# One mask for both halves of a tile, the exponential behind the routing matmuls, earlier routing for tiles 12 to 15, paired scatters

## The chip, the cores and the metric

One core of a Trainium2 chip runs the whole program in one launch. Its engines are TensorE (PE: matmuls; PEld: the weight loads in front of them), VectorE (DVE), ScalarE (ACT), GpSimd (POOL) and SyncE (SP), which issues most DMAs; POOL issues the indirect ones. Each engine works through its own list of instructions in the order in which the program wrote them. The metric is the device time of one execution in microseconds (us). The profile has a second number of this kind, the time of the profiled execution.

## The reference

Three layers follow each other over 4 x 768 tokens with 384 channels (8 heads of 48).

```python
for t in range(S):                      # attention with a decaying state, per batch and head
    cur = u * k[t] (x) v[t]
    y[t] = r[t] . (state + cur)
    state = w * state + k[t] (x) v[t]
# first mixture of experts: tokens with x @ w_skip > 0 only, the others pass unchanged
e = argmax(x @ w_gate);  gate = softmax(x @ w_gate)[e]
x = x + gate * (relu(x @ w1[e]) @ w2[e])
# second mixture of experts: every token, no residual
out = gate2 * (relu(x @ w1b[e2]) @ w2b[e2])
```

Each mixture has 8 experts of 384 x 1024 and 1024 x 384.

## The kernel before

**Attention.** The 3072 tokens are 24 tiles of 128, tile n from 0 to 23; a tile is an even and an odd chunk of 64 tokens, which lie on different partitions. XE[n % 4] and XO[n % 4] are two buffers of 128 partitions. For the even chunk, XE holds the decayed r in partitions 64 to 111, and XO is to hold the masked score matrix in 64 to 127; for the odd chunk it is the other way round. prep_a(n) (L535) makes the decayed k (KTL, L539) and r (XE, L543, both chunks at once) on DVE and r times k (RKP, L544) on POOL. prep_b(n) (L546) copies the odd chunk's r from XE into XO on ACT. amat(n) is four steps: the score matmuls (amat_a, L584 and L585, both chunks into one PSUM tile a_ps), the matmuls for the diagonal (amat_q, L593), and mask (L595), which multiplies the two halves of a_ps by a triangle, one DVE instruction into the lower half of XE and one into the upper half of XO. prep_kq (L556) makes KDE, KDO and qv on DVE. uy (L604) is the recurrence: it updates the state with one chunk and makes the output of the chunk before, uy even with XO (L617, L621) and uy odd with XE (L615, L623). evac_state (L625) copies the state from PSUM on ACT: L631 after uy even, L629 after uy odd. finish (L633) adds qv to the output on DVE. In iteration n of the loop, the program writes uy even (n), prep_a(n+3) with finish(n-1) in its middle, amat(n+2), prep_kq(n+2), uy odd (n), prep_b(n+3), and then the gate's logits of tile n-2 (gate_l, L271) and transposes of tile n-1 (gate_x, L396).

**Routing.** route (L285) turns logits into a slot for each token: transposes (L296), nine or ten small DVE steps up to the one-hot matrix ohm (L327) and its sum cs (L332), the exponential on ACT (L334), three DVE steps to the gate weight, matmuls that count the tokens ahead (rk, L344 to L348), three DVE steps to the index and the running count cum (L350 to L354). It is a generator: it yields the name of an engine, and the loop calls tick at fixed places, which lets it write its next instruction. A slot is half an iteration (in the experts: one piece of a matmul job). The first number behind the engine's name is a lag in slots; a step of another engine has lag 1 if none is given. GROUPS says which tiles are routed together and with which lag; with burst, all DVE and ACT steps that follow each other are written at one tick. Only one generator runs at a time, others queue.

**Rows to the experts.** A routed tile is scattered to its experts' rows in DRAM by indirect DMA on POOL (L276). Tiles 0 to 15 fill the first 160 rows of expert 0: in iteration 21, early_rows writes what is left of their routing, the scatters of those tiles and, behind them on POOL, the load of these rows (L933). first_T transposes them (L943) and first_1 (L949) begins the experts.

**Experts.** Jobs 0 to 7 are the first mixture's experts, job 8 and 9 the second mixture's expert 0 in two parts, then the rest. A job has slots k = 0 to 15: eight of gemm1 (L1077) and eight of gemm2 (L1100). When a job of the first mixture is done, gate_rows routes its rows for the second one during the next job; send2 issues its two scatters, one a slot. Three row buffers go round, so a load of new rows (L1040) waits until the scatters of the rows in that buffer have landed. Rows of the eighth job go into job 9, whose transposes (L1052) come from slot 13 of job 8 on.

Of the kernel before, what the change touches and what calls it, by code (L numbers as in the profile page):

```python
# [52 lines left out]
FILL = (17, {}, 6)  # L53
W_LO, W_HI = 0.7, 1.5

GROUPS = {0: (4, 2), 4: (4, 2), 8: (4, 2), 12: (4, 2), 16: (4, 0), 20: (3, 1), 23: (1, 1)}
LL, LT0 = 5, 13
PF2 = range(8, 23)
PF1 = (3, 4, 5, 6, 7, 8)
# [123 lines left out]
def attn_moe_moe_kernel(ctx: ExitStack, tc: tile.TileContext, t, out):  # L183
# [101 lines left out]
    def route(lt, X, g0, n, two, idx_out, ec):  # L285
# [43 lines left out]
        if n > 1:  # L329
            cs = rt_p.tile([128, nc_], F32, tag="cs", name="cs")  # L330
            yield "dve"
            V.tensor_reduce(out=cs, in_=ohm.rearrange("p g c -> p c g"), axis=AX.X, op=ALU.add)  # L332
        yield "act0"
        A.activation(out=ex, in_=lm, func=ACTF.Exp)  # L334
        sm = rt_p.tile([128, n, sets, 1], F32, tag="sm", name="sm")
        yield "dve0"
        V.tensor_reduce(out=sm, in_=ex, axis=AX.X, op=ALU.add)
        yield "dve"
        V.tensor_scalar(out=sm, in0=sm, scalar1=1e-9, scalar2=None, op0=ALU.add)
        yield "dve"  # L340
        V.reciprocal(out=X[:, g0:g0 + n, G1 + (0 if two else 1):G2 + 1], in_=sm.rearrange("p g s o -> p g (s o)"))
        sl = rt_p.tile([128, n, nc_], F32, tag="sl", name="sl")
        yield "pe 0" if two or len(whole) > E - 2 else "pe 3"
        T.matmul(rk, lhsT=ones[0:2, :], rhs=ecap[:, ec, c0:16].unsqueeze(1).to_broadcast([2, n, nc_]), start=True, stop=False)  # L344
        T.matmul(rk, lhsT=ones, rhs=cum[:, c0:16].unsqueeze(1).to_broadcast([128, n, nc_]), start=False, stop=False)
        for g in range(n - 1):
            T.matmul(rk[:, g + 1:n], lhsT=ones, rhs=ohm[:, g].unsqueeze(1).to_broadcast([128, n - 1 - g, nc_]), start=False, stop=False)
        T.matmul(rk, lhsT=tri, rhs=ohm, start=False, stop=True)  # L348
        yield "dve"
        V.scalar_tensor_tensor(out=sl.rearrange("p g c -> p (g c)"), in0=ohm.rearrange("p g c -> p (g c)"), scalar=-NOSLOT, in1=rk.rearrange("p g c -> p (g c)"), op0=ALU.mult, op1=ALU.add)  # L350
        yield "dve"
        V.tensor_reduce(out=idx_out.unsqueeze(3), in_=sl.rearrange("p g (s c) -> p g s c", c=8), axis=AX.X, op=ALU.min)
        yield "dve"
        V.tensor_tensor(out=cum[:, c0:16], in0=cum[:, c0:16], in1=cs, op=ALU.add)  # L354


    gens = []
# [51 lines left out]
    def attention():  # L409
        with ExitStack() as actx:  # L410
# [58 lines left out]
            def fl(x):  # L469
                return x.rearrange("p h c -> p (h c)")  # L470
# [74 lines left out]

            def prep_b(n):  # L546
                x = n % NX
                A.copy(out=fl(XO[x][0:D]), in_=fl(XE[x][0:D]))

            def prep_v(n):  # L550
                A.copy(out=fl(VSO[n % NL][64:128]), in_=fl(VSE[n % NV][64:128]))
# [17 lines left out]
                tick("dve")  # L569
                qv_t[n] = qv  # L570

            a_t = {}

            def amat(n):
                amat_a(n)
# [3 lines left out]
            def amat_a(n):  # L579
                x = n % NX  # L580
                a_ps = ps.tile([128, H, C], F32, tag="a", bufs=2, name="a_ps")
                kt_ = ktil.pop(n)
                for h in range(H):
                    T.matmul(a_ps[0:64, h], lhsT=kt_[64:128, h], rhs=XE[x][64:128, h], start=True, stop=True)  # L584
                    T.matmul(a_ps[64:128, h], lhsT=kt_[0:48, h], rhs=XO[x][0:48, h], start=True, stop=True)  # L585
                a_t[n] = a_ps

            def amat_q(n):
# [6 lines left out]
            def mask(n):  # L595
                x = n % NX
                a_ps = a_t.pop(n)
                for X, r0 in ((XE[x], 0), (XO[x], 64)):
                    V.tensor_tensor(out=X[r0:r0 + 64], in0=a_ps[r0:r0 + 64], in1=before[r0:r0 + 64].to_broadcast([64, H, C]), op=ALU.mult)
                    tick("dve")  # L600

            y_ps, u_ps = {}, {}

# [49 lines left out]
            def gate_l(n):  # L653
                g0, gn, k = grp[n]
                if k == 0:
                    lt_t[g0] = ps_g.tile([128, 512], F32, tag="lt", name="lt_ps")
                lt_ps = lt_t[g0]
                logits_T(lt_ps[:, k * 128:k * 128 + 128], xT_t.pop(n), 128)
                if k == gn - 1:
                    lt = ga_p.tile([96, 512], F32, tag="lt", bufs=2, name="lt")  # L660
                    defer.append(lambda: A.copy(out=lt[:, 0:gn * 128], in_=lt_ps[0:96, 0:gn * 128]))
                    if g0 >= EARLY:
                        deferred()
                    busy.add(g0)
                    start(gate_route(lt, g0, gn), lag=GROUPS[g0][1], burst=g0 == 20)

            busy = set()

# [57 lines left out]
            prep_kq(0)  # L726
            setup5(2)
            zero_state(0)
            fill(FILL[2])
            load_rk(3)  # L730
            load_kv(3)
            for n in range(NT):
# [3 lines left out]
                deferred()  # L736
                if n == 0:
                    prep_v(1)
                slot[0] += 1
                tick("pe ")  # L740
                fill(FILL[1].get(n, 0))
# [46 lines left out]
                if n == 0:  # L788
                    amat_a(2)
                    amat_q(2)  # L790
                    prep_a(3)
                    mask(2)
                    prep_kq(2)
                    load_rk(5)
                if n + 3 < NT:
                    prep_b(n + 3)
                    prep_v(n + 3)
# [339 lines left out]
    def work(j, k):  # L1137
# [14 lines left out]
            tick("dve")  # L1152
        if j <= E:
            if j > 1:
                send2(1 + (j == E))
            if skipped and j > 2 and k % 2 == 0:
                g = skipped.pop(0)
                scatter(xs2, idx_all[:, g, 1:2], xall[:, g], SLOTS2 - 1, "s2")
# [137 lines left out]
```

## Time and profile before

| | us |
|---|---|
| median of 3 runs | 582.07 (581.66 to 582.59) |
| the profiled execution, its own time | 586.06 |
| span of its instructions | 584.3 |
| attention, from the first uy even to the last logits | 18.8 to 157.2 |
| first expert's matmuls begin | 166.5 |
| mean granted TensorE clock, share of full speed | 0.969 |

A row of the timeline has start, duration, engine, line, operation, what it writes and reads, how many instructions are merged, and in brackets the idle time of the engine before it with what ended it. The clock has two levels, 1.2 and 2.4 GHz; a clock of 0.75 in a stretch says that it was at the lower level for half of it.

### The profile page before, as it was taken

To read this page: it belongs to the slowest core of one execution; us is meant where nothing else is said; L and a number is where in the kernel's file an instruction comes from. 1 tells how busy PE (TensorE), PEld (TensorE's weight loads), DVE (VectorE), ACT (ScalarE), POOL (GpSimd) and SP (SyncE) were. 2 spreads that over 40 slices of the span, in tenths; PEclk is the share of its full clock that TensorE was granted. 3 is DMA by queue.
4 is the path that set the end of the run, shared out by engine and by line. 5 is a ranking of instruction groups with operands and counts; after the bars stand their busy time and mean duration, and the time that the engine had idled before them with its cause. 6 is when DMAs were issued, how large, how long until landed. Compare 5 with 4: busy or idle time off the path is not lost. (4 is left out here: it accounts for less than half of the span.)

```text
span 584.3 us, 14702 instructions
## 1 busy us (share of the span) xinstructions
PE 551.1 (94%) x5947; PEld 496.8 (85%) x5948; DVE 361.2 (62%) x761; ACT 266.1 (46%) x536; POOL 207.6 (36%) x224
## 2 busy tenths in 40 slices
PE   6999898898789999999999999999999999999992
PEld 4788797787677899998989799988989898999992
DVE  7999999999536577766775536444434344455210
ACT  6344444544325654654465326443445354555320
POOL 6442234432342233688733322222231313141301
PEclk8779898999979999999999999999999999999997
DMA  7959777887523756687766533766465564742100
GB/s 153 212 144 272 233 222 206 251 271 282 191 92 113 275 174 218 203 256 227 257 207 214 165 106 111 242 206 212 165 200 167 182 231 145 260 144 81 38 16 27
DMA packets 57661, 107.67 MB, mean 184 GB/s; under 512 B 7321, under 2 KB 40958, under 8 KB 57584
## 3 DMA queue, kind: packets, MB, share of 16 engines
q1 hardware_dynamic: 51584, 94.57, 52.9%
q0 software_dynamic: 6000, 12.07, 5.6%
q8 instruction: 49, 0.80, 0.6%
q14 instruction: 28, 0.23, 0.1%
HBM read 85.86 MB, written 26.91 MB: 193 GB/s over the span
## 5 line engine op out<-in xcount | busy, mean ns | idle before, releaser
L1077 PE MATMUL g<-xh,w1h 128*128 128x240 f32 (+7 forms) x384 | 121.3, 316 | 0.0
L1077 PE MATMUL g<-xl,w1h 128*128 128x240 f32 (+7 forms) x384 | 118.6, 309 | 0.1
L1077 PE MATMUL g<-xh,w1l 128*128 128x240 f32 (+7 forms) x384 | 118.5, 309 | 0.0
L1079 DVE SCALAR_TENSOR_TENSOR hl<-g,hh 128x384 fp32r<-128x384 f32 (+5 forms) x128 | 58.7, 464 | 85.2 <-ACT hh L1078 85.1
L1100 PE MATMUL g<-w2h,hh 128*128 128x384 f32 (+4 forms) x312 | 108.5, 348 | 0.0
L1100 PE MATMUL g<-w2h,hl 128*128 128x384 f32 (+4 forms) x312 | 105.0, 337 | 0.0
L1100 PE MATMUL g<-w2l,hh 128*128 128x384 f32 (+4 forms) x312 | 105.0, 336 | 0.0
L1078 ACT ACTIVATE hh<-g 128x384 fp32r<-128x384 f32 (+5 forms) x128 | 53.4, 417 | 62.8 <-PE g L1077 61.7
L887 POOL TENSOR_TENSOR w1l<-s,w1h 128x1024 fp32r<-128x1024 f32 x14 | 33.5, 2394 | 125.5 <-issue 106.6
L1077 PEld LDWEIGHTS g<-xh,w1h 128*128 128x128 f32 x384 | 72.6, 189 | 4.2 <-DVE w1l L887 2.5
L1077 PEld LDWEIGHTS g<-xl,w1h 128*128 128x128 f32 x384 | 72.6, 189 | 1.2 <-DVE xl L1056 0.3
L1077 PEld LDWEIGHTS g<-xh,w1l 128*128 128x128 f32 x384 | 72.6, 189 | 0.9
L276 POOL DMA_INDIRECT xs<-xall,idx_all x48 | 54.3, 1130 | 31.0 <-DVE cum L354 12.8
L1100 PEld LDWEIGHTS g<-w2h,hh 128*128 128x128 f32 (+4 forms) x312 | 57.6, 185 | 4.0 <-issue 3.0
L276 POOL DMA_INDIRECT out<-rows,ids x30 | 29.1, 971 | 85.3 <-ACT rows L921 59.8
L1100 PEld LDWEIGHTS g<-w2l,hh 128*128 128x128 f32 (+4 forms) x312 | 57.1, 183 | 0.7
L1100 PEld LDWEIGHTS g<-w2h,hl 128*128 128x128 f32 (+4 forms) x312 | 56.9, 182 | 0.8
L544 POOL TENSOR_TENSOR RKP<-RK 112x512 f32<-112x512 f32 x22 | 29.7, 1348 | 74.4 <-DMA RK<-in_rk 58.0
L1056 DVE TENSOR_TENSOR xl<-xt_ps,xh 128x240 fp32r<-128x240 f32 (+7 forms) x48 | 23.0, 478 | 49.3 <-ACT xh L1055 49.2
L887 DVE TENSOR_TENSOR w1l<-s,w1h 128x1024 fp32r<-128x1024 f32 x28 | 34.4, 1230 | 21.3 <-ACT w1h L886 21.3
L887 DVE TENSOR_TENSOR w2l<-s,w2h 128x1152 fp32r<-128x1152 f32 x28 | 37.9, 1354 | 13.4 <-ACT w2h L886 13.4
L886 ACT CAST w2h<-s 128x1152 fp32r<-128x1152 f32 (+1 forms) x42 | 43.9, 1048 | 0.0
(200 smaller groups left out, 1053.2 us busy)
## 6 DMA issues: line engine op xcount, KB each, us to landing
s<-in_w1b SPq DMA_DIRECT2D x24, 512.0 KB, 3.8
s<-in_w1a SPq DMA_DIRECT2D x21, 512.0 KB, 3.9
RK<-in_rk SPq DMA_DIRECT2D x48, 192.0 KB, 4.0
KV<-in_kv SPq DMA_DIRECT2D x24, 384.0 KB, 5.1
s<-in_w2b SPq DMA_DIRECT2D x16, 576.0 KB, 4.8
s<-in_w2a SPq DMA_DIRECT2D x14, 576.0 KB, 5.8
w2r<-in_w2b SPq DMA_DIRECT2D x5, 1536.0 KB, 9.1
xs<-zrow SPq DMA_DIRECT2D x29, 194.0 KB, 4.6
```

What stands on the lines that cost most here:

```text
L276: i = P.indirect_dma_start(out=dst, out_offset=bass.IndirectOffsetOnAxis(ap=idx_col, axis=0), in_=src, in_offset=None, bounds_check=last, ...
L544: (V if n < 2 else P).tensor_tensor(out=RKP[x][0:112], in0=RK[i][:, 0], in1=RK[i][:, 1], op=ALU.mult)
L886: A.copy(out=hi, in_=x)
L887: (P if j in POOL_LO else V).tensor_tensor(out=lo, in0=x, in1=hi.bitcast(F32), op=ALU.subtract)
L1056: V.tensor_tensor(out=lo, in0=tp[:, 0:cap], in1=hi.bitcast(F32), op=ALU.subtract)
L1077: T.matmul(p, lhsT=a[:, kb, f], rhs=b[:, kb], start=(kb == 0 and i == 0), stop=(kb == KB - 1 and i == 2))
L1078: A.activation(out=hh[:, fb], in_=p[:, 0:full], func=ACTF.Relu)
L1079: V.scalar_tensor_tensor(out=hl[:, fb], in0=p[:, 0:full], scalar=0.0, in1=hh[:, fb].bitcast(F32), op0=ALU.max, op1=ALU.subtract)
L1100: T.matmul(p[0:m], lhsT=a[:, fb, r], rhs=b[:, fb], start=(fb == 0 and x == 0), stop=(fb == FB - 1 and x == 2))
```

## The change

mask writes both halves with one DVE instruction into XO; a new step mask_b copies the lower half from XO to XE and then the odd chunk's r into XO, both on ACT. The odd chunk's r now waits in a small tile xt (three buffers), which prep_b fills, and the odd score matmuls read XE. mask_b(n+2) is written behind uy odd (n) and its evacuation. In route, the matmuls rk come behind cs, then the exponential, then the index steps, then the three steps of the gate weight. The seventh expert's rows take the lag of 3 slots in front of rk that the earlier ones take. Group 12 gets lag 0 and burst. send2 issues two scatters in a slot for jobs 2 to 7 too.

```diff
-GROUPS = {... 12: (4, 2), 16: (4, 0), 20: (3, 1), 23: (1, 1)}
+GROUPS = {... 12: (4, 0), 16: (4, 0), 20: (3, 1), 23: (1, 1)}
...
-        yield "act0"
-        A.activation(out=ex, in_=lm, func=ACTF.Exp)
-        sm = ...
-        yield "dve0"
-        (sum of ex; + 1e-9; reciprocal)
         sl = rt_p.tile([128, n, nc_], F32, tag="sl", name="sl")
-        yield "pe 0" if two or len(whole) > E - 2 else "pe 3"
+        yield "pe 0" if two or len(whole) > E - 1 else "pe 3"
         (matmuls rk)
-        yield "dve"
+        yield "act0"
+        A.activation(out=ex, in_=lm, func=ACTF.Exp)
+        yield "dve0" if two and g0 >= EARLY else "dve"
         (sl, idx, cum)
+        yield "dve"
+        (sum of ex; + 1e-9; reciprocal)
...
             def prep_b(n):
                 x = n % NX
-                A.copy(out=fl(XO[x][0:D]), in_=fl(XE[x][0:D]))
+                xt_t[n] = wk.tile([64, H, C], F32, tag="xt", bufs=3, name="xt")
+                A.copy(out=fl(xt_t[n]), in_=fl(XE[x][0:64]))
...
-                    T.matmul(a_ps[64:128, h], lhsT=kt_[0:48, h], rhs=XO[x][0:48, h], start=True, stop=True)
+                    T.matmul(a_ps[64:128, h], lhsT=kt_[0:48, h], rhs=XE[x][0:48, h], start=True, stop=True)
...
-                for X, r0 in ((XE[x], 0), (XO[x], 64)):
-                    V.tensor_tensor(out=X[r0:r0 + 64], in0=a_ps[r0:r0 + 64], in1=before[r0:r0 + 64].to_broadcast([64, H, C]), op=ALU.mult)
-                    tick("dve")
+                V.tensor_tensor(out=XO[x], in0=a_ps, in1=before.to_broadcast([128, H, C]), op=ALU.mult)
+                tick("dve")
+                tick("dve")
+
+            def mask_b(n):
+                x = n % NX
+                A.copy(out=fl(XE[x][0:64]), in_=fl(XO[x][0:64]))
+                A.copy(out=fl(XO[x][0:64]), in_=fl(xt_t.pop(n)))
...
-                    start(gate_route(lt, g0, gn), lag=GROUPS[g0][1], burst=g0 == 20)
+                    start(gate_route(lt, g0, gn), lag=GROUPS[g0][1], burst=g0 in (12, 20))
...
+                if n + 2 < NT:
+                    mask_b(n + 2 if n else 1)
...
-                send2(1 + (j == E))
+                send2(2)
```

mask_b(0) is written ahead of the loop and mask_b(2) near the start of iteration 1.

## Rows read from the trace of the kernel before

**Rows 1.** The page: busy time of each engine, share of the span, instructions.
```profile
PE 551.1 (94%) x5947; PEld 496.8 (85%) x5948; DVE 361.2 (62%) x761; ACT 266.1 (46%) x536; POOL 207.6 (36%) x224
```

**Rows 2.** Windows by stage: stretch, length, busy time by engine, clock, DMA, GB/s.
```profile
59.37:83.33 23.96, 22.29 (x559) 19.79 (x559) 23.40 (x47) 10.51 (x23) 7.51 (x6) 0.93 0.77 229
...
107.48:131.59 24.11, 21.20 (x559) 18.59 (x559) 23.54 (x49) 10.56 (x23) 8.95 (x8) 1.00 0.91 273
131.59:157.23 25.64, 23.95 (x580) 20.57 (x579) 21.52 (x60) 10.34 (x23) 7.59 (x8) 1.00 0.67 236
157.23:166.48 9.25, 3.80 (x19) 2.32 (x19) 0.90 (x6) 1.67 (x4) 3.02 (x5) 0.75 0.50 166
```

**Rows 3.** Windows of single iterations: n = 8, 14, 15, 17 and 20.
```profile
66.08:72.92 6.84, 6.84 (x144) 6.16 (x144) 6.60 (x15) 3.04 (x7) 1.27 (x1) 0.75 0.71 215
102.03:107.48 5.45, 5.45 (x143) 4.79 (x142) 5.38 (x9) 3.63 (x8) 2.87 (x3) 1.00 0.65 208
107.48:114.74 7.26, 5.04 (x138) 4.42 (x137) 7.09 (x17) 2.00 (x6) 3.16 (x3) 1.00 0.92 274
...
120.39:125.36 4.97, 4.97 (x139) 4.42 (x138) 4.88 (x11) 2.98 (x6) 1.67 (x2) 1.00 0.97 288
...
138.44:143.78 5.34, 5.34 (x144) 4.71 (x144) 5.12 (x14) 3.04 (x7) 0.00 (x0) 1.00 0.80 282
```

**Rows 4.** Timeline of DVE in iterations 15 and 18.
```profile
109.74 0.55 DVE L634 TENSOR_TENSOR xall<-yp,qv 128x384 f32<-128x384 f32 x1
...
115.38 0.23 DVE L327 TENSOR_TENSOR ohm<-eq,m 128x64 bf16<-128x64 f32 x1
...
129.08 0.68 DVE L543 TENSOR_TENSOR XE<-RK,TR 112x512 f32<-112x512 f32 x1
129.68 0.68 DVE L599 TENSOR_TENSOR XE<-a_ps,before 64x512 f32<-64x512 f32 x1
...
131.08 1.45 DVE L560 TENSOR_TENSOR KDE<-KV,TKH 64x384 f32<-64x384 f32 x1
```

**Rows 5.** Timeline of ACT in iterations 14 and 15.
```profile
106.72 0.62 ACT L548 COPY XO<-XE 48x512 f32<-48x512 f32 x1
...
108.56 0.47 ACT L631 COPY VSO<-up 48x384 f32<-48x384 f32 x1 [0.68 <-PE up L617]
...
113.93 0.26 ACT L334 ACTIVATE ex<-lm 128x64 f32<-128x64 f32 x1 [4.53 <-DVE lm L315]
114.22 0.47 ACT L629 COPY KV<-up 48x384 f32<-48x384 f32 x1
```

**Rows 6.** Timeline of PE: seven places from the first tiles to job 8.
```profile
23.55 1.10 PE L593 MATMUL q_ps<-u_c,RKP 128*64 128x1 f32 x32 [0.87 <-DVE qv L568]
...
101.19 0.42 PE L271 MATMUL lt_ps<-xT,wg 128*32 128x128 f32 x6
...
102.03 0.24 PE L617 MATMUL up<-KV,KDE 112*48 112x48 f32 x1
...
161.53 0.30 PE L943 MATMUL f_ps<-ident,rows 128*128 128x128 f32 x1 [4.30 <-DMA rows<-xs]
162.84 1.61 PE L943 MATMUL f_ps<-ident,rows 32*128 32x32 f32 x5 [1.01 <-DMA rows<-xs]
...
323.01 0.17 PE L347 MATMUL rk<-ohm,ones 128*128 128x8 bf16 x1 [0.98 <-DVE ohm L327]
...
346.53 0.37 PE L1052 MATMUL xt_ps<-ident,rows 128*128 128x128 f32 x2
```

**Rows 7.** Timeline of POOL at the end of attention.
```profile
146.07 0.98 POOL L276 DMA_INDIRECT xs<-xall,idx_all  x1 [10.93 <-DVE cum L354]
...
156.93 1.14 POOL L933 DMA_DIRECT2D rows<-xs  x2 [5.74 <-DMA xs<-xall,idx_all]
```

**Rows 8.** Timeline of SP in job 8: the first load is job 9's rows.
```profile
342.96 0.88 SPq L1040 DMA_DIRECT2D rows<-xs  x2
```

**Rows 9.** Who waited for L1040's loads: us in total, times.
```profile
  PE xt_ps L1052: 1.2, 2
```

More of the change, by code (lines that the diff above doesn't have):

```diff
@@ L54 @@
 W_LO, W_HI = 0.7, 1.5
-GROUPS = {0: (4, 2), 4: (4, 2), 8: (4, 2), 12: (4, 2), 16: (4, 0), 20: (3, 1), 23: (1, 1)}
+GROUPS = {0: (4, 2), 4: (4, 2), 8: (4, 2), 12: (4, 0), 16: (4, 0), 20: (3, 1), 23: (1, 1)}
 LL, LT0 = 5, 13
@@ L332, in route @@
             V.tensor_reduce(out=cs, in_=ohm.rearrange("p g c -> p c g"), axis=AX.X, op=ALU.add)
+        sl = rt_p.tile([128, n, nc_], F32, tag="sl", name="sl")
+        yield "pe 0" if two or len(whole) > E - 1 else "pe 3"
+        T.matmul(rk, lhsT=ones[0:2, :], rhs=ecap[:, ec, c0:16].unsqueeze(1).to_broadcast([2, n, nc_]), start=True, stop=False)
+        T.matmul(rk, lhsT=ones, rhs=cum[:, c0:16].unsqueeze(1).to_broadcast([128, n, nc_]), start=False, stop=False)
+        for g in range(n - 1):
+            T.matmul(rk[:, g + 1:n], lhsT=ones, rhs=ohm[:, g].unsqueeze(1).to_broadcast([128, n - 1 - g, nc_]), start=False, stop=False)
+        T.matmul(rk, lhsT=tri, rhs=ohm, start=False, stop=True)
         yield "act0"
         A.activation(out=ex, in_=lm, func=ACTF.Exp)
+        yield "dve0" if two and g0 >= EARLY else "dve"
+        V.scalar_tensor_tensor(out=sl.rearrange("p g c -> p (g c)"), in0=ohm.rearrange("p g c -> p (g c)"), scalar=-NOSLOT, in1=rk.rearrange("p g c -> p (g c)"), op0=ALU.mult, op1=ALU.add)
+        yield "dve"
+        V.tensor_reduce(out=idx_out.unsqueeze(3), in_=sl.rearrange("p g (s c) -> p g s c", c=8), axis=AX.X, op=ALU.min)
+        yield "dve"
+        V.tensor_tensor(out=cum[:, c0:16], in0=cum[:, c0:16], in1=cs, op=ALU.add)
         sm = rt_p.tile([128, n, sets, 1], F32, tag="sm", name="sm")
-        yield "dve0"
+        yield "dve"
         V.tensor_reduce(out=sm, in_=ex, axis=AX.X, op=ALU.add)
@@ L341, in route @@
         V.reciprocal(out=X[:, g0:g0 + n, G1 + (0 if two else 1):G2 + 1], in_=sm.rearrange("p g s o -> p g (s o)"))
-        sl = rt_p.tile([128, n, nc_], F32, tag="sl", name="sl")
-        yield "pe 0" if two or len(whole) > E - 2 else "pe 3"
[L344 to L348, printed above, removed]
-        yield "dve"
[L350 to L354, printed above, removed]
     gens = []
@@ L570, in prep_kq @@
                 qv_t[n] = qv
-            a_t = {}
+            a_t, xt_t = {}, {}
             def amat(n):
@@ L728, in attention @@
             zero_state(0)
+            mask_b(0)
             fill(FILL[2])
@@ L738, in attention @@
                     prep_v(1)
+                if n == 1:
+                    mask_b(2)
                 slot[0] += 1
```

## The prediction

> **What bounds the kernel now.** I read the page first: PE is busy for 94% of the span, DVE for 62% [rows 1]. That average hides the stage of the change, so the next view is the windows by stage. From iteration 7 to 18 there are three routing groups of four iterations, of 23.96, 24.15 and 24.11 us (the second is not shown); DVE is busy for 97 to 98% of them, PE for 88 to 93% [rows 2]. Single iterations show who paces which. Iteration 17 has no routing: PE is busy for all of its 4.97, DVE for 4.88. Iteration 14 adds the logits' transposes, 5.45, and iteration 20 the rk matmuls, 5.34; PE is full in both, so they cost 0.48 and 0.37. Iteration 15, where DVE has nine routing steps, takes 7.26 with PE busy for 5.04 and DVE for 7.09 [rows 3]. PE's own floor for four iterations is thus 4 x 4.97 + 0.48 + 0.37 = 20.7, and 3.3 a group is all that a faster DVE can return.
>
> In iteration 15 ACT sat for 4.53 with the exponential, which waits for lm, and evacuated the state right behind it (114.22) [rows 5]; the next uy even needs that state. But DVE had no pause in this time, so that wait alone costs nothing.
>
> The last reading is the end of attention. POOL waits 10.93 for the indices of tiles 12 to 15, scatters from 146.07 and issues the load of expert 0's rows at 156.93 [rows 7]. PE gets the rows at 161.53 and 162.84 after waits of 4.30 and 1.01 [rows 6], and the clock over 157.23 to 166.48 is 0.75 [rows 2]. Here PE pays in full.
>
> **The mask.** On DVE the mask starts 0.60 behind XE, and the two masks take 129.68 to 131.08, 1.40. A row of 512 elements on 112 partitions takes 0.68, one on 64 partitions 0.68 too [rows 4], so partitions cost nothing and one mask on 128 takes between 0.60 and 0.70 from start to start. It saves 0.70 to 0.80; I take 0.75, 3.0 in a group. DVE's 23.54 becomes 20.5, about PE's floor of 20.7. What is left is then decided by waits.
>
> ACT gets two copies more an iteration, 0.62 each by the copy of the same length [rows 5]: 1.24. It had 0.68 free ahead of L631 in iteration 15 [rows 5], so L631 comes 0.56 later. Its reader, uy odd, stands behind amat on PE, about 2.0 behind uy even's end (4.97 less 0.84 for logits and transposes, 101.19 to 102.03 [rows 6], less two uy of about 1.07). L631 takes 0.47, so some 0.9 of cover is left and I cost the copies at nothing. Without the cover every iteration would lengthen. The score matmuls no longer wait for prep_b's copy; no row here shows that wait to cost anything, so I count nothing for it.
>
> Ahead of the loop one mask less is on DVE's chain: 0.75. In iteration 0 PE waits 0.87 for qv(1) [rows 6], behind one more mask: another 0.87. Sum 1.6; the bounds are nothing, if another wait takes their place, and 3, if iterations 1 and 2 get shorter by their mask as well.
>
> **Routing of tiles 0 to 11.** The exponential no longer stands in front of the state's evacuation. But rk now comes at the first PE tick behind cs, in iteration 15 itself, directly behind uy odd and in front of the logits, the transposes and the next uy even. PE is there 4.97 - 0.84 = 4.13 after the iteration's start. DVE begins finish at about 1.3 (uy even's 1.08, by L631's start at 108.56 [rows 5], and a little); from finish to ohm's end it takes 109.74 to 115.61 now, 5.87 [rows 4], less 0.75 for the mask: ohm is ready at 6.4. PE stalls for about 2.3 and then has 0.37 + 0.84 to do, so iteration 15 takes 7.7. The others go at PE's pace, 4.97 + 4.97 + 5.45: 23.1 for the group, against 24.1. If none of DVE's steps is stretched beside POOL (KDE took 1.45 at 131.08, where L634 with as many elements took 0.55), it is 22.4.
>
> Against it stands the clock. Behind the wait in iteration 7, iteration 8 has clock 0.75 and lasts 6.84, PE busy throughout [rows 3]: 1.7 to 1.8 over its floor. Two of the three groups have this today and the third is as long without it, so DVE hides it now; with PE in front it would show. The new stall is no shorter than today's (7.26 - 5.04 = 2.2). Middle: 22.8 x 3 + 2 x 1.7 = 71.8 against 72.2, which I round to no gain. Ends: 22.4 x 3 without drops, +5; 23.1 x 3 + 3 x 1.7, -2.
>
> **Tiles 12 to 15.** Lag 0 moves their logits' transposes in front of amat in iteration 18. They need a copy that ACT makes behind L631, about 0.47 + 0.6 late: PE loses 1.1 (0.6 to 1.4). Burst puts all DVE steps into iteration 19. The matmuls rk then hardly wait, as the nine steps come in front of the mask. A group's routing costs DVE 23.54 - 4 x 4.88 = 4.0, the rest of an iteration 4.88 - 0.75 = 4.1; so from finish at 1.3 all is done by 9.4, and without the next KTL (0.6) by 8.8. Today the scatters start 14.5 after iteration 19's start (131.59 to 146.07). From start of the scatters to the rows' use is 161.53 - 146.07 = 15.5, for the second part 16.8 [rows 6, 7], so both parts are there by 25.9. PE today is through with attention 25.64 after that start [rows 2]. I expect 26.6: group 16's rk now comes in iteration 22, in front of uy even, and waits about 0.9 for ohm; the transposes ahead of it wait 0.6 for a copy behind mask_b(23); finish(19) is late by about 1 behind the burst; iteration 19's own wait, 1.66, goes. So the waits of 4.30 and 1.01 vanish. Of the 9.25, 3.9 are left, at the lower clock; at the higher I take 2.6, a gain of 1.3, and the first matmuls of first_1 gain 1 more (window 166.48 to 180.27 at 0.92: 13.79 x 0.08 = 1.1). Sum: 5.3 + 1.3 + 1.1 - 1.0 = 6.7, between 4 and 8. Next late are the rows of tiles 16 to 23; they follow PE's transposes and move with them.
>
> **Experts.** The seventh expert's rk waits no more for ohm: 0.98 [rows 6]. A row buffer comes free one slot earlier, since its second scatter no longer queues behind others: up to the 1.2 that PE waited for L1040's loads [rows 9]. But the seventh expert's routing ends two slots later, the eighth's starts only then, and its scatters now wait for the gate weight, which comes last. Job 9's rows were issued at 342.96 and used at 346.53 [rows 6, 8], 3.6 later without a wait to be seen; two slots (one of gemm1 and the DVE steps) make the issue about 2.4 later, so PE waits about 2.2 (0 to 2.6). Net 0, from -1.5 to +2.
>
> **Sum.** 1.6 + 0 - 1.1 + 6.7 + 0 = 7.2. The profiled execution took 586.06, 1.76 over its span; 578.9 is expected of it. The median of runs is 3.99 lower, so 575 there.
>
> **Rivals.**
>
> DVE paces everything and all of its time comes back: the three groups at PE's floor, 3 x 3.3 = 10, instead of nothing, 1 us less for group 12's stall: 575 - 11 = 564. For it speaks DVE's 97 to 98% [rows 2], against it that rk waits for ohm in the same iteration. The Trainium skill, Perfetto Trace Analysis, "Identifying the Most-Contended Engine", says that the engine with the highest occupancy is the one to relieve first; by that rule this rival is the likely one. The trace agrees that this is DVE, but with a PE floor only 3.3 a group lower. Chance 0.13.
>
> The rows come no earlier: the change doesn't do what it is written for. If scatters or load take as long again as the time won, 5 of the 6.7 are lost and with a stall in each group the result is 580 to 583. For it: POOL's queue is in order and RKP(23) stands ahead of the scatters. Against: POOL stood idle for 10.93 in front of them [rows 7]. Chance 0.07.
>
> About half comes back, because clock drops follow all the new stalls or the waits in iterations 18 to 22 are twice as long: 577 to 581. Chance 0.16.
>
> Slower: ACT becomes late. mask_b stands ahead of prep_b and the next L631, and waits for DVE's mask. If it waits 1 us or more beyond the 0.9 of cover, uy odd is late in each iteration; over 21 iterations 0.35 us each undo the 7.2, and 0.5 each give 586. For it: DVE runs behind PE in each routing group. Against: mask comes before KDE, KDO and qv on DVE, amat_q and uy odd lie between on PE. The Trainium skill, ScalarE: Activation LUTs, "Rules for kernel authors", speaks for this rival: simple elementwise work belongs on VectorE, not on ScalarE. By the trace the two take the same for 512 elements, 0.62 and 0.68. Chance 0.09.
>
> **How the numbers follow.** The forecast has 0.55, its own range 570 to 578.5. Faster by more than 0.2% (1.2 us, about what a measurement of this kernel can tell from no change): 0.55 + 0.13 + 0.13 of the half case = 0.81. Same: 0.05 of the second rival and 0.03 of the half case = 0.08. Slower: 0.09 + 0.02 of the second rival = 0.11. The range that leaves out 2 in 10 reaches from 566 to 580.5.
>
> **What would show it.** In the changed profile: one mask of 0.6 to 0.7 an iteration; in iterations 7, 11 and 15 a PE wait of about 2 with rk and ohm in its row; iteration 18 a wait at L296; no wait at L943 and full clock there, scatters of tiles 12 to 15 some 5 earlier against iteration 19; no wait at L347 in job 7, a new one at L1052 in job 8. I am wrong if iterations 8, 12, 16 stay above 5.2 at full clock, if L617 or L615 wait for ACT in plain iterations, or if the wait for rows stays.

## The result and the profile after

The changed kernel took 588.27 us, median of 4 runs (587.49 to 589.23), beside 581.87 for the kernel before on the same chip (580.45 to 582.59, 4 runs): ratio 1.0114, 95% interval 1.0088 to 1.0140. It is slower by 1.1%, where 575.0 had been predicted; on two other chips the same change measured 0.999 and 1.003 (below). Medians in this document are of all runs, and ratios leave out, on both sides, the slow ones, which are more than 1.5% above the fastest run of the same kernel. The profiled execution took 587.76, as its other runs, with a span of 586.1. That of before took 586.06, 3.5 above the highest of its runs. The two traces therefore show only 1.8 of the 6.4 us.

The page of the changed kernel, busy time of each engine (compare [rows 1]):

```profile
PE 553.5 (94%) x5948; PEld 496.2 (85%) x5948; DVE 343.5 (59%) x737; ACT 293.7 (50%) x584; POOL 210.0 (36%) x224
```

DVE has lost 17.7 us of work and 24 instructions, ACT has gained 27.6 and 48, close to the 18 and 30 that the predicted 0.75 and 1.24 a tile make, and still the time rose. So the stage has to be looked at, not the engine. Windows by stage of the changed kernel: iteration 6, the three routing groups (iterations 7 to 18), iteration 19 to first_1, first_1 to the wait for the last copy of expert 0's transposed rows (the x copy, L956):

```profile
50.73:59.93 9.20, 7.64 (x142) 6.55 (x141) 5.65 (x9) 4.65 (x11) 2.92 (x3) 0.73 0.99 274
59.93:86.24 26.31, 23.79 (x560) 20.69 (x559) 19.37 (x43) 14.06 (x29) 8.14 (x7) 0.90 0.61 180
86.24:110.14 23.90, 22.34 (x559) 19.49 (x558) 19.41 (x43) 15.11 (x31) 10.56 (x9) 0.93 0.74 217
110.14:136.69 26.55, 23.68 (x559) 20.39 (x558) 20.81 (x44) 15.31 (x31) 10.95 (x9) 0.88 0.87 263
136.69:166.08 29.39, 26.48 (x598) 22.06 (x597) 18.01 (x58) 16.33 (x35) 9.63 (x10) 1.00 0.61 207
166.08:179.90 13.82, 13.37 (x80) 10.34 (x78) 8.11 (x31) 8.21 (x17) 6.55 (x5) 1.00 0.46 156
```

The same cuts of the kernel before that are not in [rows 2]:

```profile
53.73:59.37 5.64, 5.56 (x143) 4.87 (x142) 5.57 (x9) 2.54 (x6) 1.85 (x2) 1.00 0.83 234
...
131.59:166.48 34.89, 27.75 (x598) 22.89 (x598) 22.42 (x65) 12.01 (x27) 10.61 (x12) 0.93 0.62 218
166.48:181.33 14.85, 14.40 (x80) 11.37 (x78) 8.52 (x31) 8.21 (x17) 8.38 (x7) 0.93 0.32 106
```

Read the groups with PE's floor of 20.7 for four iterations in mind. What PE is busy beyond 20.7 is work at the lower clock (1.2 GHz); what the window is longer than PE's busy time is waiting. The first group has 3.1 of the one and 2.5 of the other, the second 1.6 and 1.6, the third 3.0 and 2.9. DVE is no longer full: 19.4 to 20.8. The waits are these, from PE's timeline of the changed kernel (the last bracket is the idle time and what ended it):

```profile
53.42 0.21 PE L585 MATMUL a_ps<-XE,KTL 64*64 64x64 f32 x1 [1.56 <-DVE XE L543]
66.24 0.22 PE L338 MATMUL rk<-ohm,ones 128*128 128x48 bf16 x3 [1.02 <-DVE ohm L327]
92.28 0.22 PE L338 MATMUL rk<-ohm,ones 128*128 128x48 bf16 x3 [1.56 <-DVE ohm L327]
116.55 0.24 PE L338 MATMUL rk<-ohm,ones 128*128 128x48 bf16 x3 [1.93 <-DVE ohm L327]
130.96 0.55 PE L296 MATMUL rk<-ident,lt 96*128 96x96 f32 x4 [0.94 <-ACT lt L668]
347.12 0.40 PE L1064 MATMUL xt_ps<-ident,rows 128*128 128x128 f32 x2 [2.29 <-DMA rows<-xs]
```

Two waits of the first group are not in this list, 0.56 at 72.36 and 0.95 at 78.11 (in the middle of uy odd); the trace names no releaser for them. The lower clock does not follow each wait. The first group begins at the one that iteration 6 left behind. Behind the 1.02 for ohm iteration 8 ran at full clock; the clock fell behind the 0.95 at 78.11, behind the other two waits for ohm, and, from 133.00 on, behind the 0.94 for lt:

```profile
59.93:61.00 1.07, 1.07 (x24) 1.07 (x25) 0.00 (x0) 0.48 (x1) 0.47 (x1) 0.50 0.30 106
67.26:73.18 5.92, 5.37 (x138) 4.55 (x138) 4.90 (x14) 3.27 (x8) 2.58 (x2) 1.00 0.71 228
79.62:82.00 2.38, 2.38 (x43) 2.29 (x43) 0.39 (x1) 2.25 (x6) 0.64 (x1) 0.50 1.02 317
93.85:99.73 5.88, 5.88 (x139) 5.30 (x138) 3.76 (x12) 1.64 (x4) 1.69 (x2) 0.82 0.25 81
118.20:123.91 5.71, 5.71 (x139) 5.17 (x138) 3.67 (x12) 1.64 (x4) 1.19 (x2) 0.85 0.59 200
133.00:136.69 3.69, 3.69 (x63) 2.89 (x59) 3.55 (x5) 1.44 (x3) 1.26 (x1) 0.57 0.98 319
```

The balance of the two traces goes stage by stage. Start of iteration 7: 59.93 against 59.37, 0.56 lost; the changed kernel was 3.00 ahead at 50.73 and lost 3.56 in iteration 6 (9.20 against 5.64), which begins with the wait for XE and runs on at clock 0.73. The groups: 76.76 against 72.22 [rows 2], 4.54 lost. Iteration 19 to first_1: 29.39 against 34.89, 5.50 won; the waits of 4.30 and 1.01 [rows 6] are gone. First_1: 1.03 won. From there to the end, 406.2 against 403.0, 3.2 lost: PE was busy 1.9 longer, 1.7 of it lower clock (0.78 from 347.10 to 355.00) behind the new wait of 2.29 for job 9's rows, and idle 1.3 longer, as smaller waits went in return. Sum: 1.8 lost, the difference of the spans.

What the change exchanged in the groups is best seen in PE's waits over these 72 to 77 us. The kernel before:

```profile
PE up L617 <- ACT KV L629: 3.9, 2, 2.2
PE up L617 <- ACT KV L554: 2.0, 1, 2.0
```

and the changed kernel:

```profile
PE rk L338 <- DVE ohm L327: 4.5, 3, 1.9
PE up L622 <- issue: 0.9, 1, 0.9
PE rk L296 <- ACT lt L668: 0.9, 1, 0.9
```

Before, PE waited 5.9 in three places for the state (in one for its zeroing), which ACT brought late because the exponential stood ahead of it. Now it waits 4.5 in three places for ohm.

### The profile page after: what moved, and what is told of

Read it like the earlier page. It is cut to its first block, busy times and chain, and to the rows that moved or that the text cites. A ratio compares the mean times of both kernels' runs of the same rounds, so it can differ in the third digit from the quotient of the medians.

```text
span 586.1 us, 14726 instructions
## 1 busy us (share of the span) xinstructions
PE 553.5 (94%) x5948; PEld 496.2 (85%) x5948; DVE 343.5 (59%) x737; ACT 293.7 (50%) x584; POOL 210.0 (36%) x224
## 5 line engine op out<-in xcount | busy, mean ns | idle before, releaser
L276 POOL DMA_INDIRECT xs<-xall,idx_all x48 | 56.8, 1182 | 42.6 <-DVE xall L354 11.5
L1067 ACT CAST xh<-xt_ps 128x240 fp32r<-128x240 f32 (+7 forms) x48 | 20.1, 419 | 51.9 <-PE xt_ps L1064 51.4
```

The costliest lines, as they stand in the source:

```text
L276: i = P.indirect_dma_start(out=dst, out_offset=bass.IndirectOffsetOnAxis(ap=idx_col, axis=0), in_=src, in_offset=None, bounds_check=last, ...
L1067: A.copy(out=hi, in_=tp[:, 0:cap])
```

## The experiments

Runs were made on five chips; on chip A, that of the result, the kernel before took 582, on B 595 and 597, on C 589, on D 585.5, on E 595. Runs of different chips are compared only by their ratios to the kernel before on the same chip. "M" is the mask part (prep_b, amat_a, mask, mask_b and its calls), "R" the new order in route, "G" lag 0 and burst of tiles 12 to 15, "S" two scatters a slot, "W" the bound of len(whole), which decides whether the seventh expert's rk waits 3 slots.

| run | edit | chip | median us | ratio to before, 95% |
|---|---|---|---|---|
| mask_only | before + M | B | 588.8 | 0.990 (0.986 to 0.994) |
| mask_route | before + M + R | B | 603.2 | 1.014 (1.010 to 1.018) |
| mask_route_group | before + M + R + G | B | 608.4 | 1.017 (1.012 to 1.023) |
| mask_route_att | before + M + R in attention | B | 605.0 | 1.013 (1.007 to 1.019) |
| mask_rk_later | the same, rk later | B | 596.8 | 0.998 (0.994 to 1.002) |
| mask_group | before + M + G | B | 589.1 | 0.987 (0.982 to 0.992) |
| changed_rk_later | changed, rk later | B | 595.5 | 0.994 (0.990 to 0.999) |
| changed_again | changed | C | 584.5 | 0.999 (0.995 to 1.003) |
| change_without_mask | changed without M | C | 593.0 | 1.011 (1.005 to 1.017) |
| mask_burst | before + M + burst | C | 576.8 | 0.982 (0.976 to 0.988) |
| mask_burst_send | before + M + burst + S | C | 575.9 | 0.981 (0.975 to 0.987) |
| changed_third | changed | D | 587.0 | 1.003 (0.998 to 1.007) |
| undo_rk_place | changed, rk later | D | 579.8 | 0.990 (0.987 to 0.994) |
| undo_lag | changed, lag 2 | D | 586.6 | 1.004 (0.999 to 1.008) |
| undo_expert_wait | changed, old W | D | 587.0 | 1.002 (0.998 to 1.006) |
| undo_all_three | changed, all three undone | E | 596.3 | 0.996 (0.991 to 1.001) |
| old_order_again | as mask_burst_send | E | 587.7 | 0.986 (0.980 to 0.991) |

**The parts put on one by one (chip B).** mask_only is the kernel before with this, and the copies that go with it:

```diff
-                for X, r0 in ((XE[x], 0), (XO[x], 64)):
-                    V.tensor_tensor(out=X[r0:r0 + 64], in0=a_ps[r0:r0 + 64], in1=before[r0:r0 + 64].to_broadcast([64, H, C]), op=ALU.mult)
-                    tick("dve")
+                V.tensor_tensor(out=XO[x], in0=a_ps, in1=before.to_broadcast([128, H, C]), op=ALU.mult)
+                tick("dve")
+                tick("dve")
...
+            def mask_b(n):
+                x = n % NX
+                A.copy(out=fl(XE[x][0:64]), in_=fl(XO[x][0:64]))
+                A.copy(out=fl(XO[x][0:64]), in_=fl(xt_t.pop(n)))
```

> The kernel before with the new mask alone: one 128-partition mask, the two ScalarE copies behind uy odd and prep_b's copy into a tile of its own; routing order, groups and scatters as before. Theory 1 (the loss is in the routing matmuls' new place and in the experts): the mask gains what the prediction gave it ahead of the loop and some of VectorE's 3 us a group, 574 to 580. Theory 2 (the mask itself loses, because ScalarE's copies make the state late or because PE, now in front, pays for each of its waits and for the lower clock that follows them): 582 to 588. The first reading of the trace of after favours theory 2 for iterations 3 to 10, where the longest loss (iteration 6, 9.2 us) begins at a wait for XE and not at rk.

It took 588.8 against 594.7, 5.9 us faster; the expected times were written for chip A, where 0.990 would be 576, inside theory 1. The mask wins, ScalarE's copies do not make the state late, and theory 2, which my first reading of the trace had favoured, falls. Its windows of iterations 7 to 18 and PE's waits in them:

```profile
58.11:81.54 23.43, 21.62 (x560) 18.66 (x559) 21.03 (x44) 14.56 (x30) 7.61 (x6) 1.00 0.81 236
81.54:102.96 21.42, 20.89 (x560) 18.39 (x559) 19.88 (x41) 15.67 (x32) 9.47 (x8) 1.00 0.76 224
102.96:126.38 23.42, 21.88 (x560) 18.87 (x559) 20.88 (x46) 15.27 (x31) 9.89 (x9) 1.00 0.92 271
```
```profile
PE up L624 <- ACT KV L636: 1.1, 2, 0.6
PE lt_ps L271 <- issue: 0.8, 1, 0.8
PE up L624 <- ACT KV L555: 0.4, 1, 0.4
```

With the faster mask alone, the waits for the state are 1.5 in all, and the clock is full in all three groups. The kernel before had 5.9 of these waits on chip A, and 4.0 in its own profile on this chip (before_again):

```profile
PE up L617 <- ACT KV L629: 3.0, 2, 2.4
PE up L617 <- ACT KV L554: 1.0, 1, 1.0
```

There was little left for the new order to remove.

mask_route adds the new order:

```diff
-        yield "act0"
-        A.activation(out=ex, in_=lm, func=ACTF.Exp)
-        sm = rt_p.tile([128, n, sets, 1], F32, tag="sm", name="sm")
...
         yield "pe 0" if two or len(whole) > E - 2 else "pe 3"
...
         T.matmul(rk, lhsT=tri, rhs=ohm, start=False, stop=True)
+        yield "act0"
+        A.activation(out=ex, in_=lm, func=ACTF.Exp)
...
         V.tensor_tensor(out=cum[:, c0:16], in0=cum[:, c0:16], in1=cs, op=ALU.add)
+        sm = rt_p.tile([128, n, sets, 1], F32, tag="sm", name="sm")
...
```

> Mask and the new order of the routing steps (exponential and sums behind rk), with the old group of tiles 12 to 15, the old wait of the expert routing and the old scatters. Theory 1: 3 to 6 us slower than the mask alone, from stalls of rk of 1.0 to 1.9 us in iterations 7, 11, 15 and 19 and 1.7 us of lower clock behind each. Theory 2: within 2 us of the mask alone, since the exponential's wait ahead of the state goes in return.

It took 603.2, 14.4 more than mask_only: more than twice what theory 1 expected (3 to 6). mask_route_group adds lag 0 and burst:

```diff
-GROUPS = {0: (4, 2), 4: (4, 2), 8: (4, 2), 12: (4, 2), 16: (4, 0), 20: (3, 1), 23: (1, 1)}
+GROUPS = {0: (4, 2), 4: (4, 2), 8: (4, 2), 12: (4, 0), 16: (4, 0), 20: (3, 1), 23: (1, 1)}
...
-start(gate_route(lt, g0, gn), lag=GROUPS[g0][1], burst=g0 == 20)
+start(gate_route(lt, g0, gn), lag=GROUPS[g0][1], burst=g0 in (12, 20))
```

> As mask_route, with lag 0 and burst for tiles 12 to 15. Both theories: the wait for expert 0's rows (4.30 and 1.01 before) vanishes and the clock is full behind attention, 5 to 7 us faster than mask_route. What is left to the changed kernel (588.3) is then the expert part: theory of the experts: 3 to 4 us faster than the changed kernel, as the row wait of 2.29 in job 8 and the lower clock behind it (1.7) are not there; rival: the experts are neutral, within 1 us of 588.3.

608.4, no gain where 5 to 7 were expected (the intervals of 1.017 and 1.014 overlap). On this chip there is no wait for expert 0's rows to remove: before_again, the kernel before with a profile of its own there, waits at the end of attention 1.8 for the gate's copy and not for rows.

> The kernel before, unchanged, with a profile of its own. Its first profiled execution took 586.06, its runs 580.4 to 582.6. If the 4 us are an accident of that execution (more stretches at the lower clock), a second profile shows a span near 580 and a mean clock of 0.975 or more, against 0.969; if profiling itself costs 4 us, it is near 584 again with the same waits.

It took 602.82, 8 above the median of its chip, with a clock of 0.952. It answers neither way why the first profile was 4 us long.

**Where the new order costs (chip B).** changed_rk_later puts rk of tiles 0 to 11 half an iteration later in the changed kernel:

```diff
-        yield "pe 0" if two or len(whole) > E - 1 else "pe 3"
+        yield "pe 2" if two and g0 < 12 else "pe 0" if two or len(whole) > E - 1 else "pe 3"
```

> The changed kernel with one edit: for tiles 0 to 11 the matmuls rk (and the exponential and sums behind them) come one half iteration later on PE, behind the next uy even, as before the change. Theory stall (rk in the iteration of its own ohm, and the lower clock behind that wait, are what the new order costs): the waits for ohm in iterations 7, 11 and 15 vanish, 6 to 10 us faster than the changed kernel, so at or below the kernel before (ratio 0.99 to 1.00). Rival (the order of exponential and sums, or the experts, cost it): within 2 us of the changed kernel, ratio 1.010 to 1.015.

0.994, faster than before. The next two take M and the new order in attention alone (the experts keep the old one), with rk directly behind cs and, by the same line as above, half an iteration later. soft_a is the exponential, soft_b the sum, the addition and the reciprocal:

```diff
+        if not two:
+            yield from soft_a()
+            yield from soft_b("dve0")
...
         T.matmul(rk, lhsT=tri, rhs=ohm, start=False, stop=True)
+        if two:
+            yield from soft_a()
...
         V.tensor_tensor(out=cum[:, c0:16], in0=cum[:, c0:16], in1=cs, op=ALU.add)
+        if two:
+            yield from soft_b("dve")
```

> Mask and the new order of the routing steps in attention alone; the experts' routing, the groups and the scatters as before the change. Beside mask_route (1.0139) it tells what the new order costs in the experts: by the trace of mask_route 4 to 5 us there (x copy 1.58 against 0.45 us, rk wait of the seventh expert 2.00 against 0.98 with 1.7 us of lower clock behind it), so a ratio of 1.004 to 1.008. Rival: the experts' order is neutral and the ratio stays at 1.012 to 1.016.

> As mask_route_att, but rk of tiles 0 to 11 one half iteration later, behind the next uy even. What is left of the new order is then only that the exponential no longer stands on ScalarE ahead of the state. Theory stall: at least as fast as mask_only (0.990), 0.985 to 0.992. Rival: the order of exponential and sums costs, 1.00 or more.

1.013 and 0.998. The experts' order is neutral (1.013 against 1.014 with it), against what I expected. The place of rk is worth 1.5%; but the new order with rk later is still behind mask_only, against theory stall. mask_group then takes G without R:

> Mask, and lag 0 with burst for tiles 12 to 15; routing order, experts and scatters as before the change. By the prediction 5 to 7 us faster than mask_only (0.990), so 0.978 to 0.982, as the wait for expert 0's rows goes. Rival: that wait is already gone or shorter in mask_only (its trace shows 1.9 at the logits in place of 4.30 at the rows), so the early scatters bring nothing and the wait for lt in iteration 18 is added, 0.988 to 0.995.

0.987, between the two expectations and within the intervals of mask_only. The wait for lt is there, 2.42:

```profile
122.16 0.90 PE L296 MATMUL rk<-ident,lt 96*128 96x96 f32 x4 [2.42 <-ACT lt L668]
```

**The changed kernel again, without the mask, and the old order with burst (chip C).**

> The changed kernel unchanged, on the chip of the runs beside it. If the stall of rk is the main loss, its ratio is 1.010 to 1.020, that is 1.5 to 2.5% over changed_rk_later (0.9944), which differs from it in the place of rk for tiles 0 to 11 alone. If it comes at 1.000 or less, the two chips treat the change differently and the place of rk does not explain the first result.

0.999, below the range expected: on this chip the change made no difference. The windows of its three groups, then iterations 7, 8, 11 and 12, and its waits for ohm:

```profile
56.53:80.86 24.33, 22.50 (x559) 19.92 (x558) 19.94 (x43) 15.09 (x31) 9.01 (x7) 0.93 0.77 226
80.86:105.31 24.45, 22.34 (x560) 19.60 (x559) 20.72 (x44) 15.13 (x31) 10.47 (x9) 0.93 0.74 218
105.31:130.21 24.90, 22.39 (x559) 19.58 (x558) 19.69 (x45) 14.66 (x30) 11.40 (x10) 0.93 0.87 264
56.53:64.01 7.48, 5.65 (x144) 4.85 (x143) 5.93 (x17) 5.15 (x11) 1.68 (x2) 1.00 0.81 257
64.01:70.45 6.44, 6.44 (x138) 5.86 (x138) 4.48 (x14) 1.83 (x5) 2.23 (x2) 0.74 0.61 181
80.86:88.90 8.04, 5.93 (x144) 4.97 (x143) 7.26 (x18) 5.38 (x11) 3.68 (x4) 0.94 0.84 252
88.90:94.89 5.99, 5.99 (x138) 5.41 (x138) 3.87 (x12) 1.64 (x4) 1.58 (x2) 0.80 0.28 91
```
```profile
62.99 0.22 PE L338 MATMUL rk<-ohm,ones 128*128 128x48 bf16 x3 [1.56 <-DVE ohm L327]
87.45 0.22 PE L338 MATMUL rk<-ohm,ones 128*128 128x48 bf16 x3 [2.11 <-DVE ohm L327]
111.35 0.22 PE L338 MATMUL rk<-ohm,ones 128*128 128x48 bf16 x3 [1.57 <-DVE ohm L327]
```

This is the mechanism with few side effects: each group pays one wait for ohm and then 1.6 to 1.8 of lower clock (busy 22.3 to 22.5 for a floor of 20.7); only the third has another wait of size, 0.94 for lt. The three groups take 73.7, where the kernel before took 72.2 on chip A with slow masks.

change_without_mask takes M out of the changed kernel and keeps the rest:

> The changed kernel with the two old masks and XO's copy as before, so the routing order, the group of tiles 12 to 15 and the experts' part alone. Theory (the mask gains about 1% whatever else is changed): about 1% slower than changed_again, 1.02 to 1.03. Rival (the waits show only because the mask puts PE in front; with VectorE as the pacer they are hidden): faster than changed_again, 0.995 to 1.005.

1.011, 8.5 us more than changed_again: the mask gains as much as expected, though the ratio lies below 1.02 to 1.03 because changed_again came out lower than thought. The rival, that the waits show only because of the mask, falls. The waits for ohm are 8.1 in all there, since ohm comes later still:

```profile
PE rk L338 <- DVE ohm L327: 8.1, 3, 2.8
```

mask_burst keeps the old order and lag 2, with `burst=g0 in (12, 20)`; mask_burst_send adds `send2(2)`:

> As mask_group, but the lag of tiles 12 to 15 stays 2: the transposes of their logits stand behind uy odd of iteration 18 again and VectorE's order is the same. mask_group's trace has a wait of 2.42 for lt there with 10.2 us of lower clock behind it. Theory (lag 0 buys nothing, as the steps on VectorE come at the same place, and costs this wait): 3 to 6 us faster than mask_group (0.9869), 0.977 to 0.982. Rival (the wait only moves): 0.985 to 0.990.

> As mask_burst with two scatters a slot in all of the prompt experts. By the traces of before and after the waits of the row tiles go from 0.94 and 0.27 to 0.32 and 0.39: 0.5 to 1.2 us faster than mask_burst. Rival: within 0.5 us, nothing that can be measured.

0.982 and 0.981: both beat both kernels; the send makes no difference that can be measured. That lag 2 is better than lag 0 is not shown, as the interval of mask_burst overlaps that of mask_group (0.982 to 0.992), which ran on another chip. From mask_burst, iterations 3 to 19 nearly whole in one window, and its first two groups:

```profile
34.00:131.00 97.00, 90.91 (x2417) 79.94 (x2415) 89.71 (x185) 64.34 (x128) 37.56 (x29) 1.00 0.86 258
```
```profile
57.31:79.60 22.29, 21.25 (x559) 18.54 (x558) 20.64 (x44) 15.09 (x31) 8.88 (x6) 1.00 0.80 243
79.60:100.67 21.07, 20.95 (x559) 18.48 (x558) 19.70 (x43) 15.13 (x31) 9.77 (x8) 1.00 0.83 240
```

The clock is full for 97 us on end, and the second group is 0.4 over PE's floor. The third takes 24.0, with gaps of 1.26 and 0.97 in it for which the trace names no releaser.

**One place undone at a time (chip D).**

> The changed kernel again, as the anchor of the three single edits beside it: 0.999 to 1.011 as on the two chips before.

1.003, between the two chips before. undo_rk_place is the diff of changed_rk_later:

> The changed kernel with rk of tiles 0 to 11 half an iteration later, behind the next uy even. Theory: this place holds most of the loss. In the changed kernel's trace the three groups of iterations 7 to 18 take 24.3, 24.4 and 24.9 us against 22.3 and 21.1 with the mask and the old order, so 6 to 9 us faster than changed_third. Rival: the lower clock comes behind other waits anyway and 2 us or less come back.

579.8 against 587.0, and 0.990 against 1.003: 6 to 7 us from one line, as expected, and the rival of 2 us or less falls. Its groups:

```profile
59.65:83.13 23.48, 22.55 (x560) 19.53 (x559) 19.32 (x43) 15.07 (x31) 7.54 (x6) 0.93 0.76 223
83.13:103.85 20.72, 20.72 (x559) 18.35 (x559) 19.42 (x42) 15.11 (x31) 9.21 (x8) 1.00 0.83 237
103.85:125.79 21.94, 20.91 (x560) 18.43 (x559) 20.89 (x46) 14.67 (x30) 11.07 (x9) 1.00 0.99 307
```

66.1 in all, against 73.7 in changed_again; the second group is at PE's floor, with no wait at all. The first still has 0.9 of waiting and 1.8 of lower clock. undo_lag gives tiles 12 to 15 back their lag, undo_expert_wait the old bound:

```diff
-GROUPS = {0: (4, 2), 4: (4, 2), 8: (4, 2), 12: (4, 0), 16: (4, 0), 20: (3, 1), 23: (1, 1)}
+GROUPS = {0: (4, 2), 4: (4, 2), 8: (4, 2), 12: (4, 2), 16: (4, 0), 20: (3, 1), 23: (1, 1)}
```
```diff
-        yield "pe 0" if two or len(whole) > E - 1 else "pe 3"
+        yield "pe 0" if two or len(whole) > E - 2 else "pe 3"
```

> The changed kernel with lag 2 for tiles 12 to 15 (burst kept): the transposes of their logits go back behind uy odd of iteration 18. Theory: the wait for lt (0.94) and the lower clock behind it (3.4 us at half speed, 1.7) go, 2 to 3 us faster than changed_third. Rival: the wait moves on, within 1 us.

> The changed kernel with the seventh prompt expert's rk at once behind its cs again, as before the change. Theory: the row wait of 2.3 in job 8 and 1.7 of lower clock behind it go, a wait of rk for ohm of 1 to 2 us comes back: 2 to 3 us faster than changed_third. Rival: rk's wait of 2.0 (with the exponential behind it) is followed by the lower clock in its turn, within 1 us.

1.004 and 1.002 beside 1.003: nothing, both rivals right. (undo_lag keeps the burst, so burst is not tested by it.) In undo_lag's trace iteration 18 is short and iteration 19 long:

```profile
126.92:132.37 5.45, 5.45 (x142) 4.79 (x141) 4.62 (x9) 3.33 (x8) 2.08 (x2) 1.00 1.02 335
132.37:140.11 7.74, 6.20 (x144) 5.08 (x144) 5.56 (x18) 4.06 (x9) 0.86 (x1) 0.89 1.05 381
```

What comes in the place of the row wait is seen in undo_expert_wait's own trace and in mask_route, which has the old bound too: in both the seventh expert's rk waits 2.0 for ohm, and job 9's rows are waited for 0.2 and 0.6.

**All three undone, beside the old order (chip E).** undo_all_three joins the three edits; old_order_again is mask_burst_send.

> The changed kernel with rk of tiles 0 to 11 later, lag 2 for tiles 12 to 15 and the seventh expert's rk at once. What is left of the new order is that exponential and sums stand behind rk. Theory (the waits hide one another, so undone together they are worth something): 0.980 to 0.984, level with mask_burst_send. Rival (the order itself costs, most of all in tiles 16 to 23 and the experts, where rk still stands directly behind its ohm): 0.988 to 0.992, as undo_rk_place.

> mask_burst_send again: new mask, burst for tiles 12 to 15, two scatters a slot, routing order of the kernel before throughout. 0.9806 on the chip before; 0.975 to 0.987 here if it holds, and under both the kernel before and the changed kernel.

0.996 and 0.986. old_order_again is inside its range. undo_all_three misses both of its ranges, and the theory that the three waits only hide one another falls: what is left of the new order costs about 1% on this chip. Whether that is the place of the exponential and sums, or of rk in tiles 12 to 23 and the experts, where it still stands directly behind its ohm, is not separated. Part of the cost has rows on chips B and E. At the end of attention ACT and DVE stand still together in mask_route's trace, with no releaser on this core, and PE waits 2.85 for that copy:

```profile
168.27 0.48 ACT L397 COPY xT<-tp 128x384 f32<-128x384 f32 x1 [4.43 <-remote]
168.81 0.65 PE L271 MATMUL lt_ps<-xT,wg 128*32 128x128 f32 x6 [2.85 <-ACT xT L397]
```
```profile
168.38 0.56 DVE L641 TENSOR_TENSOR xall<-yp,qv 128x384 f32<-128x384 f32 x1 [4.09 <-remote]
```

Every profile of a kernel with the new order on B and E has this pair at this place; before_again, mask_only, mask_group and old_order_again have such gaps elsewhere, of 0.2 to 6.4, and no profile of chips A, C and D has any. The stage shows what they go with: from the start of iteration 22 to the use of the x copy mask_route takes 32.6 (156.60 to 189.23) and mask_only 30.4 (150.62 to 180.97). All profiles on B and E take 32.6 to 33.4 there with the new order and 28.5 to 30.4 with the old, and those on C and D 25.3 to 25.8 with either. So 2 to 5 us of the new order's cost on B and E lie in this stage. What these gaps are is not shown.

## Why the prediction was wrong, step by step

**What bounds the kernel** was right: DVE paced the groups, PE's floor is 20.7. The reading of ACT's 4.53 wait as free while DVE has no pause holds too, but it hid a consequence: with DVE relieved the exponential's wait nearly vanishes by itself (1.5 of PE's waiting on chip B, where the kernel before had 4.0), so the new order had little to earn.

**The mask** was right: one mask of 0.68 (DVE mean 683 ns over the run) and copies of 0.61 to 0.62; no wait for them could be seen in the groups, and the rival of a late ACT falls with mask_only. Ahead of the loop 1.6 was predicted and 3.0 stood at the start of iteration 6, the upper bound; iteration 6 then lost 3.56 through the wait of 1.56 for XE and 2.1 of lower clock behind it, which no step of mine had. Measured alone the mask gives 5.9 us (B) and, on top of the rest, 8.5 (C).

**Routing of tiles 0 to 11** is the step that failed, in its term for the lower clock: "Middle: 22.8 x 3 + 2 x 1.7 = 71.8 against 72.2, which I round to no gain". The waits had the right size: three of 2.1 here and 1.1 in the next step make 7.4, and A's groups have 7.0, though only 4.5 of them for ohm (1.0 to 1.9 each). The lower clock had not. I took 3.4 for the three groups, and PE was busy 7.7 beyond its floor on A and 5.1 on C. On A two of the three waits for ohm were followed by it, as assumed. The rest came behind waits for which I had put it at nothing: 1.7 behind the 0.95 at 78.11, 1.6 behind the wait for lt, about 1 left over from iteration 6. On C it came behind all three waits for ohm. So the groups took 76.8 on A and 73.7 on C, where I had 71.8 and 1.1, 72.9. With 2.1 in iteration 6 and 1.7 in job 8 A's trace has 11.5 of lower clock at the places that the change touched, and 3.4 was priced.

The step also weighed the new place of rk against the kernel before, where the mask's gain pays for it, and did not ask what the place costs by itself. Against PE's floor (3 x 20.7 = 62.1) its sum gives 9.7; the experiment gives 6 to 7 us on D. That is about all that the mask wins.

**Tiles 12 to 15**: the waits of 4.30 and 1.01 went and the clock behind them is full: 5.50 + 1.03 = 6.5 between the two traces, where 6.7 was predicted, and the wait for lt in iteration 18 was 0.94 for 1.1. The scatters start 9.5 behind the start of iteration 19 (146.18 less 136.69) in place of 14.5, where 8.8 to 9.4 had been put. By its rows the step was right. As a gain of the runs it was not: mask_group is within the interval of mask_only, and undoing the lag gives nothing. Lag 0 moves nothing that counts: the first of DVE's steps for tiles 12 to 15 starts 2.35 behind the start of iteration 19 on A and 2.25 behind it in undo_lag.

**The offset** failed with it, and is the largest single miss: "The median of runs is 3.99 lower, so 575 there". I took the 4 us that before's profiled execution lies above its runs as common to both kernels. The changed kernel's profiled execution equals its runs (0.5 below their median). Of the 13.3 us between 575.0 and 588.3 the offset makes 4.5, the groups 3.4, the experts 3.2 and the time up to iteration 7 2.2; tiles 12 to 15 were right to 0.2. It is likely, but only argued, that the long wait for rows belongs to that one execution; no other profile on chip A can tell.

**Experts**: job 8's new wait is 2.29 for the predicted 2.2, the lower clock behind it (1.7) was left out, and the net is -3.2 between the traces where -1.5 was my bound. On D undoing it gives nothing, as rk waits instead.

Of the rivals, "DVE paces everything" had the floor right: the version without the new order comes within 0.4 of it in one group and ends at 0.981, where that rival's 564 was 0.97. "About half comes back", at 577 to 581, had the cause in its words (lower clock behind all the new stalls) and still not enough of it. Of the three signs that I had named for being wrong one came in part: on A iteration 8 took 5.92 at full clock, 0.56 of it a wait without a releaser. Iterations 12 and 16 (5.88 and 5.71) were above 5.2 too, but at a clock of 0.82 and 0.85, and I had asked for full clock. The Trainium skill, Perfetto Trace Analysis, "Identifying the Most-Contended Engine", says to relieve the engine with the highest occupancy first (in the groups DVE, with 97 to 98%); for the mask alone the runs agree, with 0.990.

**Still open**: why the change measured 1.011 on A and 0.999 and 1.003 on C and D. On A's trace there are more waits (XE 1.56, uy odd 0.9) and more work at the lower clock, but only one of its four runs has a trace. Also what the gaps on B and E are, and why the new order meets them at another place.

## What to carry to other kernels

A matmul that waits for a step of VectorE in the same iteration stops all that is queued behind it on TensorE; half an iteration later it had no wait on chip D, and that was 6 to 7 us from one line. Each wait that a change adds wants a price for the lower clock behind it too, not only those in the step that one is looking at. When an engine is relieved, look again at which waits are left before rearranging anything else: one of two edits may already have removed most of what the other was meant for. Make the sum against runs and not against one profiled execution, above all where that one is longer than every run.

## What was not expected of the hardware

What a wait costs in clock could not be read from its length. Behind each of the waits for ohm of 1.56 to 2.11 in changed_again the next iteration ran at a granted clock of 0.74 to 0.80, while mask_burst kept the full 2.4 GHz over 97 us that include waits of 0.7 to 1.6. In undo_lag a wait of 1.79 for ohm was followed by 6 us at full clock, and one of 1.57 by 10.4 us at the lower level:

```profile
63.82:74.24 10.42, 10.42 (x151) 8.63 (x150) 6.16 (x16) 3.44 (x8) 3.66 (x3) 0.50 0.74 231
```

And the chip mattered: the kernel before took 582 to 597 us on five chips. On B PE had rows of gaps without a releaser ("issue") between the single matmuls of one iteration; single gaps of this kind stand in traces of the other chips too. The kernel before there, PE's waits:

```profile
PE q_ps L593 <- issue: 2.9, 6, 0.6
```
